# Gated linear attention with a multiplicative FFN on one core: loads of k, q, v and alpha one chunk less ahead, logarithms at the beginning of the step of their sums

## The chip, the cores and the metric

The kernel runs on one core of a Trainium2 chip. The metric is the device time of one execution in microseconds (us); lower is better. Of the kernel before there are nine timed runs and one profiled execution.

## The reference, cut to what matters

Two blocks follow each other. The first is a gated recurrence for 4 batches x 8 heads, 768 steps in time and 48 values per head; the second takes its result as 3072 tokens of 384 values.

```python
state = zeros((B, H, D, D))
for t in range(S):
    state = alpha[:, :, t, :, None] * state + einsum('bhd,bhe->bhde', k[:, :, t], v[:, :, t])
    y[:, :, t] = einsum('bhd,bhde->bhe', q[:, :, t], state)

x = y.transpose(0, 2, 1, 3).reshape(B * S, H * D)   # 3072 x 384
h = ((x @ w1) * (x @ w2)) @ w3                      # d_ff = 1024
out = h @ w_out                                     # 3072 x 384
```

The weights come as 64-bit floats, and q, k, v and alpha as 32-bit floats.

## The kernel before, in words

**Chunks.** Time is cut into chunks of 128 rows: 6 for each batch, N = 24 in all. A chunk is one step `n` of the main loop. Each chunk has four inputs (k, q, v, alpha), each of 128 x 8 x 48 values, 192 KB, loaded by SyncE's queue (SP) in pieces of 192 bytes.

**What a chunk goes through.** `logs` takes the logarithm of alpha on ScalarE (line 246; from chunk 10 on, lines 250 and 251 split the result in two parts, whose buffer there is only one of). `decays` sums the logarithms along time with TensorE (line 261, or 264 from chunk 10 on) and takes two exponentials on ScalarE (267, 268). `decayed` multiplies q and k by them on VectorE (277). `transposed` turns q and k with TensorE (299), and ScalarE copies them from PSUM (301). `scores` multiplies k with q (339), and VectorE masks the product (342). `outer` makes the state's next part from k and v (311, 321). `attend_state` and `attend` make y from the state and the masked scores (358, 364); ScalarE copies it to SBUF (368), and `store` writes it to DRAM in the next step (236). Every second chunk carries the last rows of the decays through DRAM (`ends`, issued by GpSimd, lines 253, 270, 272, 285), and GpSimd multiplies the state by them (330).

**What lies between.** `convert` turns the weights from 64-bit floats into parts that TensorE multiplies: it loads `raw` tiles (181) and runs four stages on ScalarE and VectorE (189 to 210). From step 6 on, `split_x` (385 to 387) and `gate` (396 to 401, 412) begin the FFN's first product for tokens that are ready, three, three, two and no pieces per step in turn. What is left of the FFN follows the loop, and fills the time from about 190 us to the end with matmuls.

**Order.** The program is written out by hand. A tile framework puts in the semaphores, and lets an instruction pass an earlier one of its engine when it counts that the earlier one is not ready; the order on each engine is then fixed. On SP the order of the trace is that of the program.

**How far ahead.** At step n the loads are v(n+3), alpha(n+5), k and q(n+4), after step n's `store`. `logs(n+4)` stands behind `decayed(n+2)` in step n, and `decays(n+3)` at the end of the step. Chunks 0 to 4 of alpha, 0 to 3 of k and q, and 0 to 2 of v are loaded ahead of the loop. k and q have 3 buffers, alpha 3, v 5 (`AHEAD + 1`).

Of the kernel before, what the change touches and what calls it, by code (L numbers as in the profile page):

```python
# [48 lines left out]
def kernel(  # L49
# [24 lines left out]
    NG = N // G  # L74
    TG = G * C
    CW = 512
    AHEAD = 4
    LATE = 10
    assert D <= DP and DM % C == 0 and DF % CW == 0 and S % C == 0 and N % G == 0
    assert DM <= 512 and TG <= 512  # L80
# [31 lines left out]

    vs = [p1.tile([C, H, DP], FP32, name=f"v{i}") for i in range(AHEAD + 1)]
    for x in vs:
        nc.gpsimd.memset(x[:, :, D:], 0.0)

    def rows(src, n):
        b, c = divmod(n, NCH)
        return src[b, :, ds(c * C, C), :].rearrange("h p d -> p h d")

    def load_a(n):
        if n < N:
            st["a", n] = inp.tile([C, H, D], FP32, tag="ac", name="ac")
            nc.sync.dma_start(out=st["a", n], in_=rows(alpha, n))

    def load_kq(n):
        if n >= N:
            return
        st["kq", n] = inp.tile([C, 2, H, D], FP32, tag="kq", name="kq")
        nc.sync.dma_start(out=st["kq", n][:, 0], in_=rows(k, n))  # L130
        nc.sync.dma_start(out=st["kq", n][:, 1], in_=rows(q, n))

    def load_v(n):
        if n < N:
            st["v", n] = vs[n % len(vs)]
            nc.sync.dma_start(out=st["v", n][:, :, 0:D], in_=rows(v, n))
# [77 lines left out]
    def convert(steps, ahead=3):  # L214

        for _ in range(steps):
            while weights and len(begun) < ahead:
                begun.append(weights.popleft())
                next(begun[-1])
            if not begun:  # L220
                return
            x = begun.popleft()
            try:
                next(x)
                begun.appendleft(x)
            except StopIteration:
                pass
# [4 lines left out]
    def store():  # L232

        while later:
            dst, src = later.popleft()
            nc.sync.dma_start(out=dst, in_=src)
# [4 lines left out]
    def logs(n):  # L241
        if n >= N:
            return
        a = st.pop(("a", n)).rearrange("p h d -> p (h d)")
        la = st["la", n] = work.tile([C, DM], FP32, tag="la", name="la")
        nc.scalar.activation(la, a, AF.Ln)
        if n >= LATE:

            t = st["la", n] = work.tile([C, 2, DM], FP32R, tag="la2", name="la2", bufs=1)
            nc.scalar.copy(t[:, 0], la)  # L250
            nc.vector.tensor_sub(t[:, 1], la, t[:, 0].bitcast(FP32))
        if n in ends:
            nc.gpsimd.dma_start(out=ends[n][2:3], in_=a[0:1])

    def decays(n):
        if n >= N:
            return
        lc = bank()[:, 0:DM]
        la = st.pop(("la", n))
        if n < LATE:  # L260
            nc.tensor.matmul(lc, utri if n % 2 else after, la, start=True, stop=True)
        else:
            for i in range(2):
                nc.tensor.matmul(lc, sums[:, n % 2], la[:, i], start=(i == 0), stop=(i == 1))  # L264

        e = st["e", n] = work.tile([C, 2, DM], FP32, tag="e", name="e", bufs=3)
        nc.scalar.activation(e[:, 0], lc, AF.Exp, scale=-1.0)
        nc.scalar.activation(e[:, 1], lc, AF.Exp)
        if n in ends:
            nc.gpsimd.dma_start(out=ends[n][0:1], in_=e[0:1, 0])  # L270
        if n + 1 in ends:
            nc.gpsimd.dma_start(out=ends[n + 1][1:2], in_=e[C - 1:C, 1])
        load_ends(n)

    def decayed(n):
        if n < N:
            nc.vector.tensor_mul(qks[n % 3][:, :, :, 0:D], st.pop(("kq", n)),
                                 st.pop(("e", n)).rearrange("p i (h d) -> p i h d", h=H))
# [9 lines left out]
    def transposed(n):  # L288
        if n >= N:
            return  # L290
        qk = qks[n % 3]
        qkT = work.tile([C, 2, NP, C], FP32, tag="qkT", name="qkT")

        tp = [bank().rearrange("p (i j c) -> p i j c", i=2, j=NP) for _ in range(2)]
        for i in range(2):
            for j in range(NP):
                for half in range(2):
                    s = ds(DP * half, DP)
                    nc.tensor.transpose(tp[half][:, i, j, :], qk[s, i, 2 * j:2 * j + 2, :], ident[s, s])  # L299
        for half in range(2):  # L300
            nc.scalar.copy(qkT[:, :, :, ds(DP * half, DP)], tp[half])  # L301
        st["qkT", n] = qkT
# [30 lines left out]
    def scores(n):  # L333
        qkT = st["qkT", n]
        sc = [bank().rearrange("p (j c) -> p j c", j=NP) for _ in range(2)]
        for j in range(NP):
            for i in range(2):
                r = ds(DP * i, D)
                nc.tensor.matmul(sc[i][:, j, :], qkT[r, 0, j, :], qkT[r, 1, j, :], start=True, stop=True)  # L339
        ms = work.tile([C, 2, NP, C], FP32, tag="ms", name="ms")  # L340
        for i in range(2):
            nc.vector.tensor_tensor(ms[:, i].bitcast(I32), sc[i].bitcast(I32), keep_bc, op=ALU.bitwise_and)  # L342
        st["ms", n] = ms
# [3 lines left out]
    def attend_state(n):  # L347
        qkT = st.pop(("qkT", n))

        y = [bank()[:, 0:HP * C].rearrange("p (j c) -> p j c", c=C) for _ in range(2)]
        st["y", n] = y, [(half * HP + j, i, y[i][ds(DP * half, DP), j, :])
                         for j in range(HP) for i in range(2) for half in range(2)]
        if n % NCH:
            for j, i, to in st["y", n][1]:
                r = ds(DP * i, D)
                nc.tensor.matmul(to, Ts[n % 2][r, j, :], qkT[r, 1, j, :],  # L358
                                 start=(j % HP == 0), stop=False, skip_group_check=True)
# [21 lines left out]
    def split_x(g, i):  # L381
        x = st.pop(("xT", g))
        t = tr[i].tile([C, 3, KM, TG], FP32R, tag="x3", name="x3")
        st["x3", g] = t
        nc.scalar.activation(t[:, 0], x, AF.Copy, scale=1.0 - 2.0 ** -13)
        nc.vector.tensor_sub(t[:, 1], x, t[:, 0].bitcast(FP32))
        nc.vector.scalar_tensor_tensor(t[:, 2], t[:, 0].bitcast(FP32), 1.0 + 1.0 / P, x,  # L387
                                       op0=ALU.mult, op1=ALU.subtract)
# [14 lines left out]
    def gate(g, f):  # L403
        r = []
        x = [[st["x3", g][:, part, kk, :] for kk in range(KM)] for part in range(3)]
        for i, scale in enumerate((1.0, P * P)):
            r.append(gw.tile([C, TG], FP32, tag="r", name="r"))
            exact(r[-1], [[w12[:, part, i, kk, ds(f * C, C)] for kk in range(KM)] for part in range(3)], x, scale)
            if len(r) == 1:
                yield  # L410
        ab = abp.tile([C, TG], FP32, tag="ab", name="ab")
        nc.vector.tensor_mul(ab, *r)  # L412
        store_ab()
        st["ab"] = g, f, ab
# [62 lines left out]
    def run(pieces):  # L477

        for _ in range(pieces):
            if not fill:  # L480
                return
            try:
                next(fill[0])
            except StopIteration:
                fill.popleft()
# [14 lines left out]
    load_kq(2)  # L500
    load_a(3)
    decayed(1)
    load_v(2)
    load_kq(3)
    load_a(4)


    begin = {4 + 4 * g: (g, range(FH if g < 4 else KF)) for g in range(5)}
# [1 line left out]
    for n in range(N + 1):  # L510
        store()
        load_v(n + AHEAD - 1)
        load_a(n + 5)
        load_kq(n + AHEAD)
        if n:
            attend_state(n - 1)
        if n < N:
            scores(n)
        transposed(n + 1)
        if n - 2 in begin:  # L520
            g, tiles = begin[n - 2]
            split_x(g, 0)
            fill.extend(gate(g, f) for f in tiles)
        pieces = (0, 3, 3, 2)[(n - 6) % 4] if n > 5 else 0
        if n == 0:
            logs(2)
            decays(2)
            logs(3)
        early = n < 7
        convert(1, 2 if n == 0 else 3)  # L530
        advance(n)
        if n:
            attend(n - 1)
        outer(n)
        run(pieces > 0)
        if early:
            convert(1)
        decayed(n + 2)
        logs(n + 4)
        if n in begin:  # L540
            load_x(begin[n][0])
        convert(early and n > 2)
        run(pieces > 1)
        decays(n + 3)
        convert(early or n % 3 == 0)
        run(pieces > 2)
# [82 lines left out]
```

## Time and profile before

| | |
|---|---|
| median of 9 runs | 492.88 us (490.69 to 496.08) |
| profiled execution, time | 491.86 us |
| profiled execution, span from first to last instruction | 490.1 us |
| TensorE busy (matmul) | 463.2 us, 95% |
| VectorE busy | 371.0 us, 76% |
| ScalarE busy | 248.5 us, 51% |
| DMA | 79.10 MB, mean 161 GB/s |
| DMA packets | 160495, of which 104640 under 512 bytes |

Everything is one core. "Idle before" is the time that an engine stood still before an instruction, and the name behind the arrow is what ended it. SP computes nothing: its rows are issues of transfers, and the length of a row is the time that the issue took. A row of several instructions has their number behind the x. The clock is the share of TensorE's full rate that was granted.

### The profile page before, as it was taken

Reading aid. Unit: us, or ns where it says so; the run is one execution under the profiler, and the core shown is the slowest. Engines: PE = TensorE matmul, PEld = TensorE weight load, DVE = VectorE, ACT = ScalarE, POOL = GpSimd, SP = SyncE. Lnnn points to the kernel's source line nnn. Section 1 sums busy time; section 2 is a strip of 40 time slices with the busy share of each in tenths; the row PEclk is TensorE's granted clock in tenths of the full one; section 3 lists DMA queues with packets and bytes.
Section 4 is the critical chain, followed back from the end, with each engine's and each line's share of the span. In section 5 each row is a group of like instructions: output and inputs, shape, how many; then the busy total and the mean of one; then the engine's idle time right before and its main releaser. Section 6 shows DMA issues by size and latency. Waiting matters only on the chain.

```text
span 490.1 us, 9909 instructions
## 1 busy us (share of the span) xinstructions
PE 463.2 (95%) x3760; PEld 423.6 (86%) x3760; DVE 371.0 (76%) x620; ACT 248.5 (51%) x479; POOL 37.1 (8%) x83
## 2 busy tenths in 40 slices
PE   3798879999999989999999999999999999999996
PEld 1576669899998979999999988888888999999996
DVE  2679899997988685999999669676433877766771
ACT  2576667876767464555555445444222533333330
POOL 2122141112203100000000000000000000000000
PEclk9998799999999999999999999999999999999999
DMA  9999999998989864765554433320002775555511
GB/s 172 187 212 199 252 193 199 239 202 210 193 216 189 216 205 114 202 182 184 165 188 136 171 107 130 102 93 32 33 32 78 218 224 176 176 177 179 178 48 48
DMA packets 160495, 79.10 MB, mean 161 GB/s; under 512 B 104640, under 2 KB 154304, under 8 KB 160448
## 3 DMA queue, kind: packets, MB, share of 16 engines
q1 hardware_dynamic: 159168, 78.40, 62.8%
q0 software_dynamic: 1280, 0.08, 0.4%
q8 instruction: 29, 0.48, 0.4%
q14 instruction: 18, 0.15, 0.1%
HBM read 56.40 MB, written 22.06 MB: 160 GB/s over the span
## 4 chain that ended last, share of the span: by engine, by line
PE 82%; DMA 6%; DVE 5%; ACT 2%; SPq 2%; issue 2%; POOL 0%; DVEq 0%; ACTq 0%; POOLq 0%
PE bank L396 40%; PE bank L400 20%; PE bank L445 8%; PE bank L339 4%; PE bank L364 3%; DMA raw<-in_moe_w_out_dram 2%; PE bank L299 2%; PE bank L358 2%; PE bank L439 1%; DMA xT<-xd 1%; PE bank L311 1%; DMA dec<-ends 1%; DMA raw<-in_moe_w_dram 1%; PE bank L264 1%; DMA ends<-e 1%
## 5 line engine op out<-in xcount | busy, mean ns | idle before, releaser
L396 PE MATMUL bank<-x,w 128*128 128x384 f32 x768 | 159.1, 341 | 0.0
L396 PEld LDWEIGHTS bank<-x,w 128*128 128x128 f32 x768 | 134.0, 188 | 3.8 <-issue 0.5
L398 ACT ACTIVATE t<-bank 128x384 f32<-128x384 f32 x152 | 74.4, 491 | 115.1 <-PE bank L396 102.4
L401 DVE SCALAR_TENSOR_TENSOR r<-bank,t 128x384 f32<-128x384 f32 x128 | 69.3, 552 | 31.9 <-ACT t L398 26.6
L400 PE MATMUL bank<-x,w 128*128 128x384 f32 x384 | 87.4, 335 | 0.4 <-DVE x L387 0.4
L396 PE MATMUL bank<-w3o,ab 128*128 128x384 f32 x384 | 70.4, 334 | 0.0
L400 PEld LDWEIGHTS bank<-x,w 128*128 128x128 f32 x384 | 68.3, 188 | 0.8 <-issue 0.7
L396 PEld LDWEIGHTS bank<-w3o,ab 128*128 128x128 f32 x384 | 66.9, 188 | 0.0
L445 PE MATMUL bank<-wo,w3T 128*128 128x384 f32 x128 | 42.6, 486 | 0.0
L339 PEld LDWEIGHTS bank<-qkT 48*128 48x128 f32 x384 | 26.1, 204 | 14.1 <-ACT qkT L301 6.5
L339 PE MATMUL bank<-qkT 48*128 48x128 f32 x384 | 31.1, 304 | 7.0 <-ACT qkT L301 5.2
L400 PE MATMUL bank<-w3o,ab 128*128 128x384 f32 x192 | 37.1, 334 | 0.0
L445 PEld LDWEIGHTS bank<-wo,w3T 128*128 128x128 f32 x128 | 24.2, 189 | 14.9
L189 ACT ACTIVATE rest<-raw 128x512 f32<-128x512 uint32 (+1 forms) x36 | 23.4, 651 | 25.6 <-DMA raw<-in_moe_w_dram 18.9
L464 DVE TENSOR_TENSOR ab<-abl,ab 128x1024 fp32r<-128x1024 f32 x24 | 29.4, 1223 | 9.1 <-ACT ab L463 9.1
L412 DVE TENSOR_TENSOR ab<-r 128x384 f32<-128x384 f32 x64 | 35.4, 553 | 0.8
L463 ACT ACTIVATE ab<-abl 128x1024 fp32r<-128x1024 f32 x24 | 25.5, 1062 | 19.3 <-PE bank L400 18.8
L400 PEld LDWEIGHTS bank<-w3o,ab 128*128 128x128 f32 x192 | 33.6, 188 | 0.0
L342 DVE TENSOR_TENSOR ms<-bank,keep 128x512 int32<-128x512 int32 x48 | 31.1, 681 | 2.9 <-PE bank L339 2.8
L301 ACT COPY qkT<-bank 128x512 f32<-128x512 f32 x48 | 25.8, 585 | 13.0 <-PE bank L299 13.0
L194 ACT ACTIVATE power<-power,rebias 128x512 uint32<-128x512 uint32 (+1 forms) x36 | 25.2, 702 | 13.7 <-DVE power L193 13.7
L401 DVE SCALAR_TENSOR_TENSOR o<-bank,t 128x384 f32<-128x384 f32 x24 | 13.4, 557 | 22.4 <-issue 13.7
(69 smaller groups left out, 537.7 us busy)
## 6 DMA issues: line engine op xcount, KB each, us to landing
abd<-ab SPq DMA_DIRECT2D x64, 192.0 KB, 2.7
abl<-abd SPq DMA_DIRECT2D x24, 512.0 KB, 4.5
raw<-in_moe_w_dram SPq DMA_DIRECT2D x16, 512.0 KB, 3.8
xT<-xd SPq DMA_DIRECT2D x12, 576.0 KB, 4.3
raw<-in_moe_w_dram SPq DMA_DIRECT2D x24, 256.0 KB, 5.0
ac<-in_alpha_dram SPq DMA_DIRECT2D x24, 192.0 KB, 5.0
kq<-in_k_dram SPq DMA_DIRECT2D x24, 192.0 KB, 5.2
kq<-in_q_dram SPq DMA_DIRECT2D x24, 192.0 KB, 4.4
```

The source lines that it names most:

```text
L194: nc.scalar.activation(power, power, AF.Relu, scale=2.0 ** 23, bias=rebias)
L301: nc.scalar.copy(qkT[:, :, :, ds(DP * half, DP)], tp[half])
L339: nc.tensor.matmul(sc[i][:, j, :], qkT[r, 0, j, :], qkT[r, 1, j, :], start=True, stop=True)
L342: nc.vector.tensor_tensor(ms[:, i].bitcast(I32), sc[i].bitcast(I32), keep_bc, op=ALU.bitwise_and)
L396: nc.tensor.matmul(p1, w[part][i], x[part][i], start=(part == i == 0), stop=(part == 1 and i == n - 1))
L398: nc.scalar.activation(t, p1, AF.Copy, scale=(1.0 + 1.0 / P) * scale)
L400: nc.tensor.matmul(p2, w[2][i], x[2][i], start=(i == 0), stop=(i == n - 1))
L401: nc.vector.scalar_tensor_tensor(to, p2, -scale, t, op0=ALU.mult, op1=ALU.add)
L412: nc.vector.tensor_mul(ab, *r)
L445: nc.tensor.matmul(po, w3T[:, j, :], wo[:, j, :], start=(j == 0), stop=(j == KF - 1))
L463: nc.scalar.activation(t[:, 0], ab, AF.Copy, scale=1.0 - 2.0 ** -13)
L464: nc.vector.tensor_sub(t[:, 1], ab, t[:, 0].bitcast(FP32))
```

## The change

It sets `AHEAD` from 4 to 3. With it, step n loads v(n+2), k and q(n+3); alpha's load goes from n+5 to n+4. Four loads ahead of the loop go away (v(2), k(3), q(3), alpha(4), which step 0 now issues), and v has 4 buffers in the place of 5. `logs(n+3)` runs in step n just behind `transposed(n+1)`, in the place of `logs(n+4)` behind `decayed(n+2)`. The number of loads and of logarithms stays the same.

```diff
-    AHEAD = 4
+    AHEAD = 3
...
     load_kq(2)
     load_a(3)
     decayed(1)
-    load_v(2)
-    load_kq(3)
-    load_a(4)
...
     for n in range(N + 1):
         store()
         load_v(n + AHEAD - 1)
-        load_a(n + 5)
+        load_a(n + 4)
         load_kq(n + AHEAD)
...
         if n == 0:
             logs(2)
             decays(2)
-            logs(3)
+        logs(n + 3)
         early = n < 7
         convert(1, 2 if n == 0 else 3)
...
         decayed(n + 2)
-        logs(n + 4)
         if n in begin:
             load_x(begin[n][0])
```

## The prediction, made before the changed kernel was run

> **What bounds the kernel now.** I read the busy times by stretch first.
>
> ```profile
> 0.00:31.00 31.00, 19.61 (x200) 13.84 (x202) 14.38 (x26) 14.98 (x31) 6.89 (x26) 1.00 1.10 187
> 31.00:66.00 35.00, 28.14 (x401) 22.75 (x398) 30.98 (x56) 23.38 (x49) 7.46 (x15) 0.85 1.02 215
> 66.00:165.00 99.00, 96.58 (x1248) 88.20 (x1248) 89.89 (x156) 69.93 (x158) 20.97 (x39) 1.00 0.98 207
> 190.00:380.00 190.00, 190.00 (x1033) 172.27 (x1031) 145.53 (x275) 88.26 (x163) 0.00 (x0) 1.00 0.37 121
> ```
>
> The columns are PE, weight loads, DVE, ACT, POOL, clock, DMA share, GB/s. From 190 us on PE never stops and the change touches nothing, so every microsecond won or lost before that stays. From 66 to 165 us PE is idle for 2.42 of 99 us and DVE for 9.11. Up to 165 us the DMA engines are full (share 1.10, 1.02, 0.98): what is loaded earlier makes something else later.
>
> Second, the timeline of SP.
>
> ```profile
> 14.25 1.04 SPq L136 DMA_DIRECT2D v<-in_v_dram  x1
> 15.39 0.89 SPq L130 DMA_DIRECT2D kq<-in_k_dram  x1
> 16.32 0.91 SPq L131 DMA_DIRECT2D kq<-in_q_dram  x1
> 17.33 1.20 SPq L124 DMA_DIRECT2D ac<-in_alpha_dram  x1
> 18.57 1.05 SPq L136 DMA_DIRECT2D v<-in_v_dram  x1
> ...
> 22.86 3.35 SPq L181 DMA_DIRECT2D raw<-in_moe_w_dram  x4
> ...
> 104.59 0.91 SPq L236 DMA_DIRECT2D xd<-x  x2
> ...
> 120.38 1.65 SPq L131 DMA_DIRECT2D kq<-in_q_dram  x1
> ...
> 141.07 0.67 SPq L131 DMA_DIRECT2D kq<-in_q_dram  x1
> ```
>
> To 164 us each issue begins within 0.5 us of the end of the one before: SP runs through its list as fast as the queue takes it. The first four rows are the loads that leave the prologue: 14.25 to 18.57, 4.32 us. Behind them come step 0's loads and the weights' `raw`.
>
> Third, who uses the loads: VectorE's timeline, the landing time on the page, and one gap of PE.
>
> ```profile
> 29.04 0.96 DVE L277 TENSOR_TENSOR qk<-kq,e 128x768 f32<-128x768 f32 x1 [1.38 <-ACT e L268]
> ...
> 31.11 0.41 DVE L190 TENSOR_SCALAR mant<-raw 128x512 uint32<-128x512 uint32 x1
> ...
> 119.38 0.96 DVE L277 TENSOR_TENSOR qk<-kq,e 128x768 f32<-128x768 f32 x1 [0.21 <-ACT e L268]
> ...
> 140.32 0.95 DVE L277 TENSOR_TENSOR qk<-kq,e 128x768 f32<-128x768 f32 x1
> ```
>
> ```profile
> kq<-in_q_dram SPq DMA_DIRECT2D x24, 192.0 KB, 4.4
> ```
>
> ```profile
> 52.13 0.91 PE L261 MATMUL bank<-la,after 128*128 128x384 f32 x2 [2.02 <-ACT la L246]
> ```
>
> The multiplications on line 277 are in the order of the chunks: 29.04 is chunk 4, 119.38 chunk 16, 140.32 chunk 19. None waits for k or q now; they wait for the exponentials, if for anything.
>
> **The change part by part.**
>
> *Fewer loads ahead of the loop.* Since SP never waits, everything behind the four loads is issued 4.3 us earlier, `raw` at 18.6 in the place of 22.86, as long as SP finds its stores ready. They nearly always are: between the end of the ScalarE copy of x and the start of its store on SP lie 1.3 us at the shortest (x of chunk 10: copied by 103.27, stored at 104.59), then 2.4 and 2.6, elsewhere 3.3 and more. If SP waits there, the queue still holds some 4 us of work, so not all of the lead is lost. The lead is between 1.3 and 4.3 us; I take 3, nearer the ordinary step than the shortest. In the opening no store is that close, so there it is 4.3.
>
> *k and q one step later.* Chunk c takes the place that chunk c+1 had. Its q lands at the start of that issue, less the lead, plus 4.4. With a lead of 3: issue plus 1.4. Against the start of its multiplication:
>
> - chunk 12: 90.87 + 1.4 = 92.27 against 91.75, 0.52 late
> - chunk 13: 98.05 + 1.4 = 99.45 against 98.75, 0.70 late
> - chunk 16: 120.38 + 1.4 = 121.78 against 119.38, 2.40 late
> - chunk 19: 141.07 + 1.4 = 142.47 against 140.32, 2.15 late
> - chunk 20: 149.69 + 1.4 = 151.09 against 149.57, 1.52 late
> - chunk 21: 155.23 + 1.4 = 156.63 against 156.10, 0.53 late
> - chunk 22: 160.54 + 1.4 = 161.94 against 160.75, 1.19 late
>
> Chunks 10, 11, 14, 15, 17 and 18 are 0.8 to 3.7 early. The late ones stand behind long steps and in short ones: a step without gate pieces takes 4.2 us (117.90 to 122.11), little more than one load takes to land. The sum is 9.0 us on VectorE. Behind the waiting multiplication are queued, in VectorE's order, the mask of the scores (line 342), the split of x (386, 387) and the gates' second read of PSUM (401); the transposes of PE wait for the multiplication itself, but they follow 2.7 us and more after its end, so they cover nearly all of this. The queue behind it is what reaches PE. VectorE's idle time of 9.11 us takes up some; as it is spread and partly ahead of the late places (1.41 and 1.02 us at 116 and 118), I take half, 4.55. Cost: 9.01 - 4.55 = 4.5 us on PE. The ends: with a lead of 4.3 the lateness is 2.2 us and the idle time swallows it, 0; with 1.3 it is 22.2 us, less all 9.1 of idle, 13.1.
>
> *The opening.* Chunk 4's q is issued at 30.77 - 4.3 = 26.5, lands at 30.9, and is wanted at 29.04: 1.8 late. Chunks 5 to 9 land 0.7 to 3.4 before they are wanted. Against this, the second weight piece, whose first VectorE stage runs from 31.11 to 32.46 and is followed by 0.95 us of waiting for POOL, is there 4.3 us earlier and can fill the 1.06 and 1.38 us for which VectorE stands at 27 and 28 us. I take 0; the ends are 1.8 us lost, and 4.3 gained if the whole opening moves up by what the queue gives.
>
> *Alpha and the logarithms.* 24 logarithms of 0.53 us remain. Their move changes little on ScalarE, since the order in the trace is already nearly that of the change: in step 5 the logarithm stands at 51.54, behind the copies of the transposes at 50.60. Alpha's tightest is chunk 17: issued at 116.40 - 3, landing 5.0 later at 118.4, then logarithm, cast and difference (0.53, 0.51, 0.56) until 120.0, and its sum is due at 121.56. Cost 0, with -0.5 to 1.2 as ends (the difference to alpha being landed without a lead). v is read at least a step after it lands, and the fifth v buffer's clearing on POOL (0.2 us) is at no end of a chain: 0.
>
> *The clock.* A new gap of PE can also cost clock. After the gap of 2.02 us shown above, the granted clock was 0.50 from 54 to 58 us, and 16 matmuls on line 339 took 2.08 us where they take 1.16 at full clock; after the gap of 1.84 at 61.8 it stayed at 1.00. So one gap of 2 us may cost about 3 us more (6 us at half rate) or nothing; I take nothing, because the gaps that I foresee lie between full stretches, like that of 0.99 us at 151.5, after which the clock was 1.00.
>
> The Trainium skill ("TensorE: Matmul & The Clock Gate", Part 1) says that the gate closes after an idle window of some 3.4 us; by that, as an estimate, no stall foreseen here would cost clock, and the gap of 2.02 us above would not have either, but the rows show that it did.
>
> Sum on the profiled execution: 491.86 + 4.5 + 0 + 0 = 496.4. That execution is 1.0 below the median of the runs, 492.88, so the forecast is 492.88 + 4.5 = 497.4.
>
> **The rivals.** Half a per cent, 2.5 us, is about what a measurement of this kernel can tell from no change.
>
> *Faster: the weights come sooner.* VectorE is 89% busy from 31 to 66 us, and much of it is conversion of weights. It stands idle for about 6 us between 15 and 33.4 us, when only one weight piece is there. If the pieces that come 4.3 us earlier fill that, the opening ends up to 4.3 us sooner, and the half clock of 52 to 60 us (some 3 us) may vanish too: 492.9 - 4.3 = 488.6, down to 485.6. For it: the idle time is there, and the rest of the opening is VectorE's own work. Against it: the chain between 20.7 and 33.4 us goes through POOL's small transfers (4.03 and 6.03 us), which the weights don't shorten. It decides if chunks 12 to 22 are less than 3 us late in sum, a lead of about 4.
>
> *No change: the two cancel.* A lead of 4.3 leaves 2.2 us late, swallowed, and the opening's gain is eaten by chunk 4: 492.9, give or take 2.
>
> *Much slower: the lead is 1.3 us.* SP is held at the stores of x in each long step, k and q are 22.2 us late in sum, PE gets 13.1: 506.
>
> That the change doesn't do what it says holds for its second half: the logarithms stand where they stood, as said above; this is in the sum already.
>
> **How the numbers follow.** The forecast has 0.46, faster 0.27, no change 0.16, much slower 0.11. Its own range is 495.5 to 502, from half the cost to one lost stretch of clock on top. The range for 8 in 10 goes from 488, which leaves out a part of the faster case, to 504. Faster by over 0.5%: 0.27; within 0.5%: 0.16; slower: 0.57.
>
> **What would show it.** In the changed profile `raw` is issued near 18.6 us, and line 277 waits for "DMA kq" at chunks 16, 19 and 20, with a gap of 1 to 3 us each; PE's idle time between 66 and 165 us rises from 2.4 to about 7 us, and the split of x in steps 14 and 18 begins later. The prediction is wrong if no multiplication waits for a DMA, if the framework's order moves masks and gates ahead of the late multiplications so that nothing stands behind them, or if the first gate (line 396, now at 65.73 us) comes more than 2 us earlier.

## The result, and the profile after

The changed kernel takes 498.63 us (median of 16 runs, 496.15 to 502.82) against 493.37 us of the kernel before in the same job (51 runs). The ratio is 1.012, with a 95% interval of 1.0097 to 1.0144: slower by 5 to 6 us. The profiled execution took 501.84 us, 3.2 above the median, with a span of 500.1; that of before was 1.5 below its median. So the 10.0 us between the two profiles overstate the difference between the kernels, and sizes below that come from single profiles are to be read with that in mind. Medians and ratios leave out the runs that fell in a slower state of the chip: two of `e2_alpha_and_logs`, one of `f1_before_kept_warm` and one of the kernel before.

The same stretches, with the same columns (PE, weight loads, DVE, ACT, POOL, clock, DMA share, GB/s):

```profile
0.00:31.00 31.00, 19.05 (x220) 13.18 (x220) 17.84 (x34) 17.63 (x36) 6.81 (x25) 1.00 1.11 191
31.00:66.00 35.00, 24.86 (x313) 19.75 (x312) 29.65 (x50) 20.71 (x44) 7.64 (x14) 0.73 1.01 215
66.00:165.00 99.00, 95.08 (x1178) 86.54 (x1178) 82.35 (x141) 66.26 (x145) 18.01 (x33) 0.94 0.92 191
190.00:380.00 190.00, 189.39 (x1117) 173.06 (x1116) 149.50 (x280) 89.56 (x167) 0.00 (x0) 1.00 0.38 122
```

From 66 to 165 us VectorE is busy for 82.35 us in the place of 89.89, and up to 31 us for 17.84 in the place of 14.38: a part of its work now comes sooner. PE is busy for less time in each of the first three stretches. In the second and third it gets through fewer matmuls (313 for 401, 1178 for 1248), so more of its work is left behind 165 us. The last row is at full clock in both.

The order on the queue is the foreseen one. This is SP's timeline, with `raw` at 18.37 in the place of 22.86:

```profile
18.37 2.45 SPq L181 DMA_DIRECT2D raw<-in_moe_w_dram  x4
```

The multiplications of chunks 4, 16 and 19 in VectorE's timeline, which began at 29.04, 119.38 and 140.32 before:

```profile
32.94 0.95 DVE L277 TENSOR_TENSOR qk<-kq,e 128x768 f32<-128x768 f32 x1
...
129.71 0.94 DVE L277 TENSOR_TENSOR qk<-kq,e 128x768 f32<-128x768 f32 x1
...
150.22 0.95 DVE L277 TENSOR_TENSOR qk<-kq,e 128x768 f32<-128x768 f32 x1
```

All three are later, and none has a bracket: VectorE did not stand idle ahead of them. No multiplication in the whole profile waits for a transfer. Of the logarithms the first three do, in both kernels, and two late ones, for 1.8 us together (before: one, 0.7 us). The multiplications stand at a later place in VectorE's order, behind other work: 180 instructions stand ahead of chunk 16's in the place of 167, and 205 ahead of chunk 19's in the place of 200.

PE waits for logarithms instead, as its timeline shows for the sums of chunks 8 and 9:

```profile
54.33 1.65 PE L261 MATMUL bank<-la,after 128*128 128x384 f32 x2 [1.50 <-ACT la L246]
...
65.06 1.65 PE L261 MATMUL bank<-la,utri 128*128 128x384 f32 x2 [3.13 <-ACT la L246]
```

ScalarE's timeline at the second of them:

```profile
63.87 0.72 ACT L194 ACTIVATE power<-power,rebias 128x512 uint32<-128x512 uint32 x1 [1.68 <-DVE power L193]
64.50 0.51 ACT L246 ACTIVATE la<-ac 128x384 f32<-128x384 f32 x1
```

Alpha of that chunk had been issued at 52.80. An alpha takes 4.3 us to land in the median, but this one took longer: its landing is at 60.2 in the trace, 4.3 us ahead of the logarithm. (`o1_two_logs_ahead`, below, where that logarithm stands first and waits for the transfer until 60.33, agrees.) The logarithm stands behind a stage of the weights that itself waits 1.68 us for VectorE. And VectorE's timeline over the same time:

```profile
60.29 1.35 DVE L386 TENSOR_TENSOR x<-xT,x 128x1152 fp32r<-128x1152 f32 x1
61.55 1.35 DVE L387 SCALAR_TENSOR_TENSOR x<-x,xT 128x1152 fp32r<-128x1152 f32 x1
...
63.09 0.41 DVE L190 TENSOR_SCALAR mant<-raw 128x512 uint32<-128x512 uint32 x1
...
67.35 0.95 DVE L277 TENSOR_TENSOR qk<-kq,e 128x768 f32<-128x768 f32 x1
```

Between 63.09 and 67.35 lie six of the seven instructions of one weight piece, and only then the multiplication of chunk 8. Counted along VectorE's order, this many weight instructions (lines 190 to 210) stand ahead of the multiplication of a chunk:

| chunk | 4 | 5 | 6 | 7 | 8 | 9 | 10 | 11 | 12 |
|---|---|---|---|---|---|---|---|---|---|
| before | 7 | 21 | 26 | 35 | 42 | 47 | 54 | 60 | 63 |
| changed | 17 | 26 | 35 | 42 | 48 | 55 | 61 | 63 | 63 |

Seven instructions are one piece; by their durations in the timeline they take 4.3 us. In chunks 4 to 10 the changed kernel converts about one piece ahead of where the kernel before did, and from chunk 12 on the two are level. The first split of x, too, stands ahead of chunk 8's multiplication and not of chunk 9's.

The other new wait is VectorE's part of the logarithms. VectorE's timeline at chunk 17, then PE's:

```profile
125.24 1.35 DVE L386 TENSOR_TENSOR x<-xT,x 128x1152 fp32r<-128x1152 f32 x1
126.51 1.28 DVE L342 TENSOR_TENSOR ms<-bank,keep 128x512 int32<-128x512 int32 x2
127.71 1.35 DVE L387 SCALAR_TENSOR_TENSOR x<-x,xT 128x1152 fp32r<-128x1152 f32 x1
128.98 0.55 DVE L251 TENSOR_TENSOR la<-la,la 128x384 fp32r<-128x384 f32 x1
```

```profile
129.58 0.69 PE L264 MATMUL bank<-la,sums 128*128 128x384 f32 x1 [1.29 <-DVE la L251]
```

The subtraction stands behind the split of x and the masks, in the step in which its sum is due. PE waits so at chunks 13, 17 and 21 (1.20, 1.29, 1.20 us). In the kernel before this subtraction was at the same place among the others (127.19), but for the chunk after, and nobody waited.

### The profile page after: what moved, and what is told of

It is laid out like the page before. It is cut to its first block, busy times and chain, and to the rows that moved or that the text cites. A ratio compares the mean times of both kernels' runs of the same rounds, so it can differ in the third digit from the quotient of the medians.

```text
span 500.1 us, 9923 instructions
## 1 busy us (share of the span) xinstructions
PE 468.7 (94%) x3760; PEld 428.2 (86%) x3760; DVE 372.4 (74%) x620; ACT 250.2 (50%) x479; POOL 37.2 (7%) x82
## 4 chain that ended last, share of the span: by engine, by line
PE 79%; DVE 8%; DMA 5%; SPq 2%; issue 2%; ACT 2%; POOL 0%; DVEq 0%; POOLq 0%; ACTq 0%
PE bank L396 38%; PE bank L400 19%; PE bank L445 8%; PE bank L339 4%; PE bank L364 3%; DMA raw<-in_moe_w_out_dram 2%; DVE ms L342 2%; PE bank L299 2%; PE bank L439 1%; PE bank L358 1%; DMA ends<-e 1%; DVE x L386 1%; PE bank L261 1%; DMA raw<-in_moe_w_dram 1%; PE bank L264 1%
## 5 line engine op out<-in xcount | busy, mean ns | idle before, releaser
L339 PEld LDWEIGHTS bank<-qkT 48*128 48x128 f32 x384 | 27.8, 217 | 10.4 <-issue 4.4
L339 PE MATMUL bank<-qkT 48*128 48x128 f32 x384 | 33.1, 319 | 3.5 <-ACT qkT L301 2.9
L401 DVE SCALAR_TENSOR_TENSOR o<-bank,t 128x384 f32<-128x384 f32 x24 | 13.4, 556 | 22.4 <-issue 13.7
```

The costliest lines, as they stand in the source:

```text
L401: nc.vector.scalar_tensor_tensor(to, p2, -scale, t, op0=ALU.mult, op1=ALU.add)
```

## The experiments

**The theories.** L: the loads come too late, and engines wait for transfers. S: the logarithms in their new place come too late on ScalarE, and PE waits for them. Q, called O from the fifth run on: the engines get another order, and it is this that costs, whatever is ready. C: PE's gaps bring stretches at half clock, and these are the loss. After the first look at the profile L stood badly, since no multiplication waited for a transfer.

Every time below is compared with the kernel before on the same chip in the same job. To see where the profiled executions part, I also give how much later than in the profile of before the mask of the scores (line 342) begins in chunk 8 and in chunk 19, and the start of the first gate (line 396).

| kernel | ratio | 95% interval | chunk 8, us | chunk 19, us | first gate at |
|---|---|---|---|---|---|
| before | 1 | | 0 | 0 | 65.7 |
| the change | 1.012 | 1.0097 to 1.0144 | 3.8 | 10.0 | 71.8 |
| `e1_kqv_only` | 1.013 | 1.0109 to 1.0151 | 8.1 | 11.4 | 75.5 |
| `e2_alpha_and_logs` | 1.0177 | 1.0139 to 1.0215 | 9.4 | 12.4 | 77.1 |
| `e3_logs_only` | 1.0086 | 1.0054 to 1.0117 | -1.1 | 1.0 | 64.7 |
| `e4_kqv_and_logs` | 1.0182 | 1.0145 to 1.0219 | 6.7 | 14.0 | 73.4 |
| `p1_change_in_old_order` | 1.0038 | 1.0010 to 1.0066 | 1.8 | 2.9 | 67.3 |
| `p2_before_in_new_order` | 1.0163 | 1.0126 to 1.0201 | 5.2 | 11.6 | 73.3 |
| `f1_before_kept_warm` | 0.9956 | 0.9925 to 0.9987 | -2.1 | -1.1 | 63.4 |
| `f2_after_kept_warm` | 1.0126 | 1.0080 to 1.0172 | 4.8 | 10.8 | 71.6 |
| `o1_two_logs_ahead` | 1.012 | 1.0082 to 1.0157 | 4.8 | 11.2 | 72.9 |
| `o2_three_subtractions_ahead` | 1.0082 | 1.0057 to 1.0106 | 3.7 | 5.8 | 71.9 |
| `o3_both` | 1.0069 | 1.0041 to 1.0096 | 4.5 | 6.8 | 71.8 |
| `v1_split_behind_chunk9` | 1.0088 | 1.0055 to 1.0122 | 7.3 | 8.9 | 72.8 |

### The parts of the change, one by one

Only k, q and v one chunk less ahead; alpha and the logarithms as before:

```diff
-    AHEAD = 4
+    AHEAD = 3
-    load_v(2)
-    load_kq(3)
```

> Only k, q and v are loaded one chunk less ahead; alpha's loads and the logarithms stay as before. Theory L (late loads): the cost comes from k and q landing late, so this kernel has all of it, ratio to before about 1.012. Theory S (ScalarE's order): the cost comes from the logarithm of alpha, whose load is a step later, standing on ScalarE behind a weight stage that waits, and PE waiting for its sum; then this kernel is like before, 0.997 to 1.003. Theory Q (the queue's order in the opening): the weights' pieces come earlier and the order on every engine is another one; then it lies between, 1.003 to 1.009.

Measured 499.55 us, 1.013: the ratio that L had named, without L's waits. What has grown is PE's wait for VectorE's product, and that product itself waits for no transfer. PE's waits up to 200 us (total, times, longest; before 6.5, 3, 3.4):

```profile
PE bank L299 <- DVE qk L277: 13.7, 6, 4.5
```

Only alpha one chunk less ahead, and the logarithms at the beginning:

```diff
-    load_a(4)
-        load_a(n + 5)
+        load_a(n + 4)
-            logs(3)
+        logs(n + 3)
-        logs(n + 4)
```

> Only alpha is loaded one chunk less ahead and the logarithm stands at the beginning of the step of its sums; k, q and v as before. Theory L: k and q are in time, 0.997 to 1.003. Theory S: all of the cost, about 1.012, with waits of PE line 261 for the logarithm of 5 us and more in sum between 20 and 75 us (before 2.4). Theory Q: between, 1.003 to 1.009.

Measured 501.8 us, 1.0177, more than any of the theories had. The same view (before 6.8, 3, 4.4; the longest is the same one, in the first microseconds of both):

```profile
PE bank L261 <- ACT la L246: 12.9, 7, 4.4
```

Only the place of the logarithms (the last three lines of that diff):

> Only the logarithms' place in the program is moved; all loads as before. By theory S in the form that the place counts, 1.005 to 1.012. By theories L and Q, and by the prediction, which held the move for no change: 0.997 to 1.003.

Measured 497.61 us, 1.0086, in S's range for the place alone. Its opening is a little faster than that of before (-1.1 us at chunk 8). At chunk 19 it is 1.0 us behind and at chunk 20 it is 4.0.

The change, but with alpha loaded as far ahead as before:

> The change, but with alpha loaded as far ahead as before. Theory L: 1.012 (k and q are late as in the change). Theory S in the form that alpha's later load counts: 0.997 to 1.003; in the form that the place in the program counts: as the logarithms alone. Theory Q: as k, q and v alone.

Measured 502.35 us, 1.0182, above what each theory had. Each part alone costs as much as the whole or more, or nearly so: 1.3, 1.8, 0.9 and 1.8% against 1.2%. In the two with later loads of k and q no multiplication waits for them (in `e3_logs_only`, with the loads of before, two do, for 1.57 and 0.83 us), so L falls as the main cause; and costs of late data or of late logarithms would add up. Costs of another order need not, because the order of VectorE and ScalarE is another one in each of these programs.

### The order and the loads taken apart

In the next two kernels the loads are those of one kernel, and the instructions of VectorE, ScalarE, TensorE and GpSimd are held in the order of the other. The lists are long; the means is short:

```diff
+def pin(tc):
+    for text in ORDER:                       # one list for each engine
+        ...
+        for before, this in zip(names, names[1:]):
+            tc.add_manual_dep(made[this], before, info, reason="order")
```

> The change as it is (three chunks ahead, alpha four, logarithms at the beginning), but with the instructions of VectorE, ScalarE, TensorE and GpSimd held in the order that they have in the kernel before. O (the time went into the other order of the instructions): 492 to 495 us, ratio 0.997 to 1.004, PE idle near the 23.1 us of before, raw still issued near 18.4 us, and half-clock time back near 10 us. L (the data come too late): 498 us or more, ratio at least 1.010, with multiplications or logarithms that wait for DMA kq or DMA ac. If both matter the ratio falls between 1.004 and 1.010.

> The loads of the kernel before (four chunks ahead, alpha five) with the instructions of VectorE, ScalarE, TensorE and GpSimd held in the order that they have after the change. O: 497 to 500.5 us, ratio 1.008 to 1.015, first gate 5 us or so later than in before, ACT la again the longest waits of the triangular products. L: 492 to 495 us, ratio 0.997 to 1.004, since no datum is late. A ratio over 1.015 would say that the order costs more than the change and that the smaller lead gives some of it back through the earlier raw.

The change's loads in the old order: 495.4 us, 1.0038, within O's range. The old loads in the new order: 501.9 us, 1.0163, a little above it; the interval does not tell whether the order costs more than the whole change. No kernel was held in its own order unchanged, but `o1_two_logs_ahead` below, held in its own with two instructions moved, has the ratio of the change, so holding an order seems to cost nothing by itself. The order carries most of the loss, and the smaller lead by itself 0.4%. Here, where the order is held, the late data can be seen; the first kernel's VectorE, ScalarE and PE:

```profile
31.50 0.96 DVE L277 TENSOR_TENSOR qk<-kq,e 128x768 f32<-128x768 f32 x1 [5.56 <-DMA kq<-in_q_dram]
```

```profile
61.26 0.52 ACT L246 ACTIVATE la<-ac 128x384 f32<-128x384 f32 x1 [1.72 <-DMA ac<-in_alpha_dram]
```

```profile
61.83 1.37 PE L261 MATMUL bank<-la,utri 128*128 128x384 f32 x2 [3.13 <-ACT la L246]
```

Chunk 4's q holds VectorE for 5.56 us, and alpha of chunk 9 holds the logarithm, which holds PE. The logarithms of chunks 5, 14, 17, 20 and 21 wait for alpha too, 1.1 to 3.6 us each, but PE's waits show none for these. No multiplication behind chunk 4 waits for k or q, that of chunk 16 neither:

```profile
122.23 0.96 DVE L277 TENSOR_TENSOR qk<-kq,e 128x768 f32<-128x768 f32 x1
```

Its q lands at 121.8 in the trace, just where the prediction had put it. But the multiplication now begins 2.85 us later than before, so it is not late any more: the work lost further ahead has already made room.

### The clock

Between 40 and 74 us the changed kernel's PE ran at a mean clock of 0.70. In the next two kernels extra products of 128 x 256 values, whose results are not used, fill some of PE's gaps; the order of everything else is held.

> The kernel before in its own order, with 20 extra 128x256 products on PE, whose results are not used, put where PE has its gaps at 41, 50 and 62 us (5, 8 and 7 of them). C (gaps of 1 to 2 us bring half-clock stretches of 3.4 and 6.8 us, which cost half their length where PE is busy): the two half-clock stretches of before go, up to 5.1 us gained, 488 to 491.5 us, ratio 0.990 to 0.997. Rival (the opening runs at the pace of VectorE, ScalarE and the transfers, so that PE's rate there costs nothing): 492.5 to 494.5 us, ratio 0.998 to 1.003, with the half-clock time gone and PE idle risen by as much.

> The changed kernel in its own order, with 37 extra 128x256 products on PE, whose results are not used, where its PE has gaps at 31, 43, 49, 53 and 62 us (6, 8, 4, 6 and 13 of them). C: most of the 20 to 27 us at half clock up to 72 us goes, up to 8 us gained against the changed kernel, ratio to before 0.998 to 1.006. Rival (opening at the pace of the other engines): ratio to before 1.009 to 1.015 as without them, half-clock time gone and PE idle risen by as much.

With 20 products in the kernel before: 492.47 us, 0.9956, a small gain, by its ratio in C's range, and the only kernel here that is faster than both; its first gate comes at 63.4 in the place of 65.7. With 37 in the changed kernel: 500.87 us, 1.0126, none that shows. The rows from 40 to 74 us, the changed kernel first, then the same with the products:

```profile
40.00:74.00 34.00, 25.69 (x288) 20.94 (x285) 28.48 (x47) 20.64 (x42) 7.35 (x13) 0.70 1.06 216
```

```profile
40.00:74.00 34.00, 27.50 (x341) 22.93 (x342) 30.38 (x51) 21.18 (x46) 7.22 (x13) 0.90 1.04 221
```

The clock rises from 0.70 to 0.90, and the first gate comes at 71.6 in the place of 71.8. By these two profiles PE's rate does not set the pace in that opening; the half-clock time is what the waits leave behind. For the changed kernel the rival held, for the kernel before C. The interval of 1.0126 (1.0080 to 1.0172) would still hide a gain of the size that the kernel before had.

### Few instructions moved

Now the changed kernel in its own order, with two to seven instructions moved.

On ScalarE, the logarithms of chunks 8 and 9 ahead of the weight stage:

```diff
 ScalarE, chunk 9
+L246 log
 L301 L301 L189 L368 L368 L194
-L246 log
```

> The changed kernel with every instruction of the engines held in its own order, except two: on ScalarE the logarithms of chunks 8 and 9 stand ahead of the weight stage that they stood behind (by 3 and 6 places). O (the place of the logarithms in the order is what the opening loses): the gaps of PE at 52.8 and 61.9 us (1.50 and 3.13 us) go and with them some half-clock time; first gate 3 to 5 us sooner than 71.8 us, ratio to before 1.001 to 1.007. Rival (the opening is bounded by VectorE, so that another wait takes the gaps' place): first gate moves by less than 1.5 us, ratio 1.009 to 1.014.

Measured 500.33 us, 1.012: nothing. PE's timeline shows what took the place of the two waits for the logarithms:

```profile
59.91 1.12 PE L299 MATMUL bank<-ident,qk 64*128 64x64 f32 x16 [2.44 <-DVE qk L277]
...
69.44 1.12 PE L299 MATMUL bank<-ident,qk 64*128 64x64 f32 x16 [2.84 <-DVE qk L277]
```

The gaps were 1.50 and 3.13 us and are 2.44 and 2.84 now, at the next thing that VectorE owes. And the logarithm of chunk 9, moved ahead, meets its transfer:

```profile
60.33 0.52 ACT L246 ACTIVATE la<-ac 128x384 f32<-128x384 f32 x1 [0.95 <-DMA ac<-in_alpha_dram]
```

The rival held: the opening is not paced by the place of these two logarithms.

On VectorE, the subtractions of chunks 13, 17 and 21 ahead of the masks or the split's second pass:

```diff
 VectorE, chunk 17
 L386
+L251 subtraction
 L342 L342 L387
-L251 subtraction
```

> The changed kernel in its own order, except three instructions on VectorE: the subtractions of the logarithms (L251) of chunks 13, 17 and 21 stand ahead of the masks and the last split of x that they stood behind. O: the three gaps of PE of 1.2 to 1.3 us at 97, 128 and 161 us go (3.7 us), and the half-clock stretch at 129 us (3.4 us lost) may go too: 3.7 to 7.1 us gained against the changed kernel, ratio to before 0.998 to 1.005. Rival (the splits and masks are as urgent, so that PE waits for them instead): ratio 1.009 to 1.014 with a new wait for DVE x or DVE ms of the same size.

Measured 497.58 us, 1.0082, between the two ranges. The profiles agree: chunk 19 is 5.8 us behind before and not 10.0, while chunk 8 is where it was. VectorE's subtraction and PE's sum at chunk 17:

```profile
126.07 0.55 DVE L251 TENSOR_TENSOR la<-la,la 128x384 fp32r<-128x384 f32 x1
```

```profile
127.92 0.44 PE L264 MATMUL bank<-la,sums 128*128 128x384 f32 x1
```

The wait is gone, with the half-clock stretch behind it. Waits of 0.64 us for the mask and 0.54 us for the product came up there, so not all of it was won. By the ratios it is 0.4%, the intervals overlapping a little.

> Both edits at once: five instructions of the changed kernel moved. O: the gains add up, 7 to 11 us against the changed kernel: ratio to before 0.990 to 1.000, since the earlier weights had put the changed kernel 1 to 2 us ahead up to 50 us. Rival: 1.009 or more; if only one of the two edits pays, the ratio is that one's.

Measured 497.67 us, 1.0069, not told apart from the last kernel. Against `o1_two_logs_ahead` the three subtractions again gain 0.5%: only one of the two edits pays, and they don't add up to a gain over before.

The last kernel adds the split of x to this, moved behind the multiplication (the expectation calls it chunk 9's; counted from 0, as elsewhere here, it is chunk 8's):

```diff
 VectorE
-L386 L387
 L319 L190 L193 L196 L197 L199 L209
 L277 multiplication of chunk 8
+L386 L387
```

> The kernel with both edits (two logarithms and three subtractions ahead, ratio 1.0069) and two instructions more moved: on VectorE the two passes of the first split of x (L386, L387, 2.5 us) stand behind the multiplication of chunk 9 (L277) instead of ahead of it and of the weight stage before it, as in the kernel before. O (VectorE's order is what the opening loses: the longest gap there is PE's wait for qk of chunk 9, 3.46 us): that gap falls to about 1 us, first gate 69 to 70 us instead of 71.8, ratio to before 1.000 to 1.004. Rival (the weight stages of the earlier raw fill VectorE so that the split's place does not matter): gap and first gate as before to 1 us, ratio 1.005 to 1.010.

Measured 498.55 us, 1.0088: a miss for O. The gap of PE that was to fall from 3.46 to about 1 us is 3.85. Its VectorE, then its PE:

```profile
63.67 0.36 DVE L319 COPY T<-bank 128x192 f32<-128x192 f32 x1 [2.56 <-PE bank L311]
...
68.31 0.95 DVE L277 TENSOR_TENSOR qk<-kq,e 128x768 f32<-128x768 f32 x1
```

```profile
69.41 0.74 PE L299 MATMUL bank<-ident,qk 64*128 64x64 f32 x16 [3.85 <-DVE qk L277]
```

Where the split had stood VectorE now idles for 2.56 us, because the next instruction in its order, the state's copy, waits for PE. The weight piece between 63.9 and 68.3 stands behind that copy, and the multiplication behind the piece. The split had only filled a hole. The ratio lies in the rival's range.

**What follows, and what stays open.** Shown: the order of the engines' instructions carries most of the loss (1.0163 with the old loads, against 1.0038 for the new loads in the old order); the late data by themselves cost 0.4%; three subtractions behind splits and masks cost about 0.4% of it; raising the clock of the changed opening gains nothing that can be measured. That one weight piece too early on VectorE is the rest, some 4 us at chunk 8, is read from the counts and from the last timeline, and not shown: no kernel moved the whole piece back without also taking back the rest of the order. It is not the whole story of the opening either: `e2_alpha_and_logs` has 42 weight instructions ahead of chunk 8's multiplication, as many as before, and loses most there, with PE waiting for logarithms.

## Why the prediction was right or wrong, point by point

- **The time and the sign were right** (forecast 497.4, measured 498.63), and the way there was not, so that the number came so near is luck. The main term, 4.5 us of lateness between 66 and 165 us, is the step that failed: the runs show 0.4%, some 2 us, for late data and the rest for the order of the instructions, which the prediction had at nothing.
- **`raw` near 18.6**: right, 18.37.
- **k and q late in chunks 12 to 22.** No multiplication waited for a transfer, which the prediction had named as what would make it wrong, and its reason too: the framework's order. The late data did not become waits, because the multiplications had been given later places (chunk 16 at 129.71, chunk 19 at 150.22), with splits and masks ahead of them. Even with the order held, lateness was paid elsewhere: 5.56 us at chunk 4, for which the prediction had 1.8 and charged nothing, and at alpha of chunk 9 (1.72 us), where PE stood too; at k and q of chunks 12 to 22 none. The landings there were foreseen well (chunk 16: 121.78, found 121.8). What failed is the sum: each chunk's lateness was taken against the starts of before and added up to 9.0 us, but from chunk 8 on the whole work is already 1.8 to 2.9 us later, and that covers the largest single lateness, 2.40. In all 0.4%, some 2 us, against 4.5.
- **SP never waits.** That was read from before, and the lateness was worked out from one fixed lead. After the change SP has gaps (it is still from 110.4 to 114.2 us, ahead of a store of `ab`, and from 124.4 to 127.6, ahead of a store of x).
- **PE idle between 66 and 165 us**: foreseen 7 us, found 3.9. Of that 3.7 are the three waits for line 251. The stretch of half clock behind the second of them, 6.8 us long, comes on top.
- **The opening at 0, with ends of -4.3 and 1.8.** It lost 6.1 us at the first gate and 3.8 us at chunk 8 in the profile, beyond the end. The rival "the weights come sooner" had the right cause and the wrong sign: the weights did come sooner and VectorE did convert them sooner, up to 31 us it was busy 3.5 us longer, but ahead of the chunks' own work, for which PE was waiting; that this is the cause is read from the counts, not shown. At chunk 5 the changed kernel was still 0.9 us ahead.
- **Logarithms at 0, "nearly that of the change".** Mis-sized: the place of the logarithms alone costs 0.9% (`e3_logs_only`). The step looked at the first half, where the order is nearly the same, and not at lines 250 and 251, where the reserve between the subtraction and its sum goes away. In the changed kernel PE waits for it three times; in `e3_logs_only` once (chunk 21's, 1.34 us, with 3.4 us of half clock behind it), just where it falls behind. The end of 1.2 us was for one chunk's alpha, not for waits on VectorE.
- **The clock at 0**: right in effect for the opening, where raising the clock of the changed kernel gains nothing that shows, though that the gaps would bring so much half clock was not seen. In the later stage one stretch of half clock stands behind the gap at chunk 17.

## What to carry to other kernels

Where a framework orders the instructions by when it counts their data to be ready, a change of a load's lead is a change of the order on every engine; compare the order first, by counting what stands ahead of the instructions that the bounding engine waits for, and only then look for data that come late. To tell the two apart, hold the order of one kernel and use the loads of the other: the two crossed kernels said more here than four that took the change apart. Late loads are not to be added up chunk by chunk when the queue does not wait and the work does: what one has delayed, the next finds done. And filler work that raises a low clock tells in one run whether the clock is a cause or only the trace of waits that are there anyway.

## What the runs showed of the hardware

A gap of PE of 1.29 us can be followed by half clock for longer than it lasts. The stretch behind PE's wait at chunk 17, by the columns of the first fence:

```profile
129.30:136.10 6.80, 6.52 (x69) 5.75 (x71) 4.07 (x7) 3.09 (x7) 1.88 (x4) 0.50 1.14 198
```

It ran at 0.50 for 6.8 us, with PE busy for 6.52 of them. In six profiles with this gap, five have such a stretch behind it; of twelve gaps of 1.20 us at chunks 13 and 21 in the same profiles, one has. The half-clock stretches in all these profiles are near 3.4, 6.8, 10.2, 13.7 or 27.3 us long, multiples of 3.41. The Trainium skill ("TensorE: Matmul & The Clock Gate", Part 1) gives a free-running window of that length, which agrees with the lengths; that a whole idle window is needed does not agree with the 1.29 us here.

What singles out the gap at chunk 17 was not tried, but the traces say something of it. Within each profile all half-clock stretches from 10 us on begin on one grid of steps of 3.41 us. Here are the step ahead of the stretch above, and for `e2_alpha_and_logs`, the one of the six without a stretch, the two steps that share its gap:

```profile
125.87:129.28 3.41, 2.18 (x37) 1.41 (x33) 3.41 (x5) 2.15 (x6) 0.28 (x2) 1.00 0.57 99
```

```profile
130.80:134.21 3.41, 2.54 (x43) 1.77 (x39) 3.41 (x4) 2.61 (x7) 0.55 (x1) 1.00 0.82 148
134.21:137.62 3.41, 2.75 (x47) 2.33 (x49) 3.11 (x6) 1.59 (x4) 1.39 (x2) 1.00 0.88 165
```

In the first PE is idle for 1.23 us of one step; in the second the gap is cut in two, 0.87 and 0.66. Over the steps from 24 to 190 us of all 14 profiles, every full-clock step with more than 1.75 us of idle time was followed by half clock and none with less than 1.05 was; in between both occur. So it seems to be the idle time summed within a step that counts, and not the length of one gap. This is read from the traces, and no kernel was made to test it.
